# A fused attention and gated-GLU kernel on one core: the whole order of work is replaced by another, with four buffers of exponentials fewer and two down-weight tiles more

## The chip, the core and the metric

The kernel runs on one core of a Trainium2 chip. A core has five engines that run their own instruction queues side by side: TensorE (PE in the profile, its weight loads apart as PEld), VectorE (DVE), ScalarE (ACT), GpSimd (POOL) and SyncE (SP), which here issues the DMAs. The metric is the time of one execution on the device in microseconds, lower being better.

## The reference

For 2,048 tokens of width 512 the kernel computes two branches of the same input `x` and mixes them with a gate per token:

```python
g = sigmoid((x * gate_w).sum(-1, keepdims=True))
# branch a: 32 heads of 16, one shared key head and one shared value head
q = (x @ wq) as (32 heads, 2048, 16);  k = x @ wk;  v = x @ wv
p = softmax(q @ k.T * 16 ** -0.5)
a = (p @ v, heads side by side) @ wo
# branch b: width 1792 inside
b = (sigmoid(x @ w_gate) * (x @ w_up)) @ w_down
out = g * a + (1 - g) * b
```

## The kernel before, in words

**Tiling.** The tokens are cut into 4 blocks of 512 and the heads into 8 groups of 4, so there are 32 *units* of attention (a block of queries, four heads). A unit has 16 *chunks* of 128 keys. Operands of most products are split into a high and a low part (the tiles with two halves, `hl`, `w`, `wd`, `x`, `qs`), so that three products of parts make one product of full accuracy.

**Kinds of work on TensorE.** Three kinds use only 64 of the 128 rows of the array, and two of them run at once, one on the top rows and one on the bottom rows:

- *maxima* (letter m, line 1139): scores of a part of the queries against 512 keys into one of 8 PSUM banks, from which VectorE takes the maximum of each row (line 1141). 64 of them make a unit.
- *scores* (s, line 1148): the scores of 128 keys for 512 queries, with the maximum subtracted in the product; ACT makes the exponential of the bank into a tile `p` (line 1150). 64 make a unit.
- *feed-forward steps* (f, line 1113): products of the gate, the up, the down and the attention's output weights, summed in a bank over several steps. ACT takes a gate bank out (line 1122), VectorE an up bank (line 1128), and the parts of the output are gathered either by VectorE (line 1070) or by ACT into a tile of its own (line 1089), which POOL then adds (line 1092).

Three kinds use all rows of the array:

- *values* (V, line 1012): the four exponential tiles of one chunk times the values, summed in a bank over the chunks that follow one another. When a run of V ends, ACT copies the bank out (line 1019); if it is not the first run of the unit, POOL adds the copy to the unit's sum (line 1026).
- *projections and transposes at the start* (G, lines 870 and 943), and *turning the maxima* (T, line 998).

The maxima run some units ahead of the scores, and the feed-forward steps fill the rest.

**What sets the order.** The string `ORDER` lists all of TensorE's work by hand, one character a step. V, G and T are full-array steps. A hexadecimal digit is a pair of half-array steps: its upper two bits are what the top rows do, its lower two what the bottom rows do (0 nothing, 1 a maximum, 2 scores, 3 a feed-forward step). So `e` is a feed-forward step on top and scores below. A dot is a moment of waiting. `State.step` reads a character and emits the instructions:

```python
if code in "VGT":
    if not self.full:
        self.now += IN
    self.full = True
    ...
else:
    if self.full:
        if self.sum is not None:
            self.release()
        self.now += OUT
```

`release` is the end of a run of V: it emits the copy of the sum and, for a later run of the unit, POOL's addition. Which bank a step takes, when weights are loaded and split, and which engine gathers a part follow from clocks that `State` keeps for each engine, in units of which a pair takes 100. The constants are the paces of that model: `RED` is a maximum on VectorE, `EXP` an exponential on ACT, `COPY` and `SCALED` copies on ACT, `LATE` and `LATE_A` the time from a matmul to the start of VectorE or ACT on its bank. They do not reach the chip; they decide only what is emitted when. In the built program each engine carries its instructions out in the order in which they were emitted, and waits on semaphores for what it needs.

`PB` is the number of `p` tiles; `can_s` lets no score be issued while that many exponentials are held, and each V gives four back. `DB` is the number of `wd` tiles, which hold split down weights, attention-output weights and, at the start, parts of the third block of `x`.

Of the kernel before, what the change touches and what calls it, by code (L numbers as in the profile page):

```python
# [680 lines left out]


ORDER = (
    "GGGGGGG555G55G555.G55........5G55GG555GGG555G55G555GG55G557G777fddfffdffdfd7GT7dffff7ffd75Gdefffdfe7edef6f6f9fbf"
    "7b7b7bbdfedef97bf9fbffeeaaVV555VVV7b7b7bfbdedbdbf9fededededbf7bfb76fef67effd9VVVV5b7b7bfbfe7eeddbf6fedeedef7f6fe"
    "7bdbdbf6fbf5VTVV555VVVV7b7bb7fedbdbde7bfededeedef7e7fedb7bbd7bffd6V569VV97fbdbb7f9fe7ef6fbdededee7fb7f6f9fb7edef"
    "f75VVV59aVV97fbe7dbfbdbf6f9fbdededee7fe7f9f9fbdffd7775VVTVV655VVV76fef97efedee7f6f9fb7b7bbdfdbfb7edbdbfefed5VV56"
    "6VVV5bfbf97bf6fbf9f9fededeedef77e7bfb7be7ffddd5VVVV7b7bb7b7fededef9fe7edeede7ff6f9fe7e7bf9fbfaTV5a5VVVV5bbb77fef"
    "9fbdef6dbfedeede7f7efe7edb7eff7775VV599VV595VVV5eeedfbdf6fb7edbfbdb7bb7bdff97bfef9fe7edfd5VV566VVVdededefe7e7e7b"
    "dbfb7b7b7bbdfedf6feedf9ff7775VTVV596VV9dfbf6bdfb7bdbf9ef7ededee7ff6fed6febffb7bb9V555VVVVV5e9ffef6fbdef6e7bdfb7b"  # L690
    "7bbdfedfb79feed7bffd6V695VV569VV5a5VTVdedeedfe7e7e7bbdfb7b7b7bbfddbfbd6fede7efbfaV599VV5bb7fbb7fe7eedf9f6fededee"
    "f7b7fed6fe7dfd7777VVV599VV5ededefefb7e7e7bfbdb7b7bbdfedf9fbede7ff75f5VVVV966V5efeedbfb77b7bfedbddd7TVV999V9b77bf"
    "fededeedb7fefbb5VV566VV695VV5bfbf6f9f6fbde7b7efededee7fedbf76fbbdbfdbf5VV659TVV5eedfe7bfe7bf6dedbfb7b7bbfdf6f9f9"
    "fef6fedf75VVVVVVV7b7bbddef9fb7e7efbdeeeded7ffe7bf6fede7b7f5bV995VV5bbfbd7efb7bdef9fe7ededee7ff6fbdb7ebdf7ff56VVV"
    "TVVde5eefbdfb7afd7bfed7b7bbbfd7bedf6fedefb7fd6V595VVVVV7bdef9f6fb7ef97bfbdedeede7f7bf6f9fee7fbdbfaV5aaVV569VV959"
    "VV97bfb7f6f9feb7defe7edeede7ff6bfde7efb5bffa7TVV59aVVVVVV5efbf6defedb7b7edefb7bb7bfdf9fb7bdeedf6ff5dVVV5bb7bfb7f"
    "bd6fef9fededeeddfb7bbf76fef6fbfee6V9a9VV5a9VVVV5b7bbfefdb7af7defbdedeede7fb7f6fb7bf6fed9fdV555VVTVV97b7bff6f9fb7"
    "eedf6fedeede7ff67bfedefe7f7776VV999VVVV9dfeed7bfb7eededfb7b7b7bbdfedfb79fef6def7f5VVV555VVVdedeedfe7e7bf97efb7bb"
    "7b7bdf7bfb7b7eeeddfdddVTVVV5bbfdbf6f9fb7bf9efdeddeedbfb7b7fe7e7beffed5VVVV7b7b7bfededb7bf9fedededee7f7bf6fbb7f6d"
    "effd5VVV566VV5eefdef6fbdbf97ef9fb7b7bbfddbfe7b7bdefedbddTVV665VV569VV5b7bbff6fedef97bf6fdedeeef77efbde7bf9fe77d7"  # L700
    "VVVVVV5efededbfb7ef9f6fe7b7b7bbfddeedf9fef9fb7bfaV569VV699VVV5bb7fef6fede7ededbfb7bb7bfd7ebdf6fef9fbdfe5V566VV95"
    "6TVV595VVV79b7bfdef9fb7be7fededeedef77ee7f9fbbdf6fbfaV656VVV5efedbf9f9fbf6f6edfb7bb7bfdf9efde7bb7fdfdd5VV665VVVT"
    "V7b7bdbdef6fbf9edbf7ededee7ff67bfedefefb797bVVVdedefe7b7b7b7bfbdeefd5VV6ddefefb7b7b7bf9fefed9VVVVVV7b7edbdbfe7ed"
    "edef6fb7b7b7fedbfbd9fbf5ffddd5VVV677b7bfbfedef9dbfe7eeddedbfbf7b7b7bfedede7dTV665VV566VV9a6VV5eeddefefb76fbdbfe7"
    "b7b7bbfddef9fedbf6bf7fd9V56aVVVV5efe7edef6fbf97ef9fb7b7b7fededef6fdfbdb7bf5VVV595VVV59effbf6f6f9fef6defb7b7b7bfd"
    "bfed9fe7bffded6V569VTV659VVVVde7bf97ef9fb7e7bbfdededeef77bbdf6fbf6defbfaV5a9VVV97bfb7b7fed9fbf6fedededeef7e7f6f9"
    "fe7bfdf775VVTV5a5VV95aVVV59bffbe7f9fe7bbdfe7ededee7f7eefde7bf6fbfbb6VVVV5ededefbf9fef6f6fb7b77bbbdfdeedfbdee7fbf"
    "b76V9a6VV6aaVVV959VV9dfbf6def6f6fef9fe7b7b7b7efedfed9fbdfff7755VVVTVV5ededefbfed9fb7efb7b7b7bbdfedf9f9fe7bff57dd"
    "VV569VV67fedbbdfe7ede7efe7bb77bbfdf9f9fbbd7efedfd5VVVVVV5bbb77fef9f6fff9fededeed7efb7af7def9fff7755VVVV7b7bb7bdf"
    "bdee7dbfedededee7fb7fb7b7ef9fedfd5VVTVV7b7bb5fef9fbf6edef7ededee7f7efb7bde7bfedf79V5aaVV56aVVV566VV5ededefbf9fee"  # L710
    "7f9fb7b7b7bbfddeefedfb79fff575VVVV5efbdef6f9f6fedbf9fb7b7bbfdedfb76fedefdf779VTVVV5eededeffe7b7b7ef9fb7b7bbfdf9e"
    "f7bdbf6fdddf6VVV566VVV97bfbd7efbdbbd7eef7ededeef7f9fb7af7bd7effe5V96aTV569VV596VVV96aVV6eddeefdfb7bedf6fb7b7b7b7"
    "efededfedef9bf7bbbV966VVVV5eededfbfed6fbbdfb7b7bb7bdfdbf6fedbedfe7f75VVVV5b7bfedefedeed7be7fb7b7bbdfdbdbfafedf7d"
    "7f5dVVVV699V9b77bffededeed7bf6f77dTVV659VV977bfbfededede7bfefbb6V655VVVV7b7b5bfef9fbf9f9fedededeef77ee7fb7bdb7ef"
    "fd5VV5a5VV5efee77efbdbf9f6def7bbb7bfdb7fbde7eedfbfee5VTV566VVVV5ededefbf6fedbb7fe7b7b7bbdfdefededbf9fb7f76V959VV"
    "956VVV5bbfed7bf9fbe7dbf6fededeef77bfb7bdbdbfefed5VVVTV977bb7fef6fbbdbdfededeede7f7ef6fb7e7bfbdfd6V5a5VVVVV5b7bfe"
    "def9fe7bb7bdfededee7fe7efde7ef9bbf777VV596VVVV5edefef9f6f9fef6fb7b7bb7bdfedfed9fe7bbfd9f7V596VV59aVVVV7b7b7bf9f9"
    "fee7edf6fedeede7f7efedbdbb7fff575VTVV5efedb7bf9fafd7efedb7b7bbdfbdbf7e7ef9fefee6V9a9VV69aVV659VV97b7fbf9fe7be7ed"
    "e7fedeedef7e77bfb7b77fdddddVVV595TVVVV7b7bdeb7f9fef6dbf6fedeedef7f9bf7e7bedbfdf75VVV7b7bbdf9fedbf6f9ffedededb7bf"
    "b7b7be7fedefed5VVVVVV5bb7bf7bfed6fbf6fededeedef7b7fede7ebfd7f775VVTV995VVVde6fb7bdfbd6fef6defb7b7bbfdf9fe7edbedf"  # L720
    "efbb5VVV6dfb7bf9fb7bbd7edefedeedef7f6e7fe7bfddd777bVV959VVVV67bfeddef6febdf6fbdb7b7bbfdf6edfbf9fb6ffee9V596VTVVV"
    "VV5b7b7bfef9f9fbf6fedededee7fe77bf6fedefb75f7VVV6dedfeedfb7bdbe7fbdb7bb7bdfdbfedb7ef6fbdfd5VVVVVV5efef6f6fbdbf6f"
    "9efdb7b7bbfdb7dbfbdef6efdfd6V656VV956VVd9fbf6e7fedef6defb7b7bb7bdfbdfed6fbf9fe7efaTV595VVVVV5bfedb7efb7ede7efedb"
    "7bb77fbdef9f9fef9f6ff5eV665VVVV5ededefbfed6fb7bf9fb7b7bbdfbde7f9febd7efee7VTV99aVV5a9VVV5b7bfbfededede7efbfbabVV"
    "6a6VVVV7b7bbfdedededef6fbb7f5VV7b6fdbdefb7bbdf6fe7ededeef7e7edf6fbfbdb7bbeV9a9VVVV696VV5eedef7ef9fb7bf6edfb7bb7b"
    "fddbbfd6fbfbfeede6VaaaTVVVVVVfbbfeffbbfeeeeeeffffffbbffffbaffeabfeVVbbbbffffbfaaVVaaeeVVeeaaVVaaaVVaaaVVa.aaVVaa"
    "VaaVV...............Vcccccccccccc"
)


# [516 lines left out]
```

## Time and profile before

| | |
|---|---|
| median of 3 runs | 1588.57 us (1587.4 to 1588.57) |
| the profiled execution | 1589.17 us, of which the span from first to last instruction is 1587.0 us |
| granted TensorE clock | 0.999 |
| TensorE busy | 1578.4 us, 12,950 matmul records |
| VectorE busy | 1357.7 us, of which maxima 1256.0 |
| ACT busy | 1233.2 us, of which exponentials 1035.4 |
| POOL busy | 788.7 us |

The page of the profile gives each engine's busy time and the chain of work that ended last. The grouped lines name a line of the kernel, the engine and the operation, the tiles out and in with their shapes, the count, then the busy time, the mean length of one in ns, and the engine's idle time just before such instructions with what ended it. A row of the timeline gives the start, the length, the engine, the line and how many like instructions were merged. The matmuls of a pair overlap each other and the next pair, so lengths of matmuls do not add up; differences between starts do. In the program's records a V counts eight matmuls.

### The profile page before, as it was taken

Reading aid. Unit: us, or ns where it says so; the run is one execution under the profiler, and the core shown is the slowest. Engines: PE = TensorE matmul, PEld = TensorE weight load, DVE = VectorE, ACT = ScalarE, POOL = GpSimd, SP = SyncE. Lnnn points to the kernel's source line nnn. Section 1 sums busy time; section 2 is a strip of 40 time slices with the busy share of each in tenths; the row PEclk is TensorE's granted clock in tenths of the full one; section 3 lists DMA queues with packets and bytes.
Section 4 is the critical chain, followed back from the end, with each engine's and each line's share of the span. In section 5 each row is a group of like instructions: output and inputs, shape, how many; then the busy total and the mean of one; then the engine's idle time right before and its main releaser. Section 6 shows DMA issues by size and latency. Waiting matters only on the chain.

```text
span 1587.0 us, 33642 instructions
## 1 busy us (share of the span) xinstructions
PE 1578.4 (99%) x12950; PEld 1026.2 (65%) x12950; DVE 1357.7 (86%) x2320; ACT 1233.2 (78%) x2426; POOL 788.7 (50%) x662
## 2 busy tenths in 40 slices
PE   9999999999999999999999999999999999999998
PEld 7776666666666566666656666666666666676663
DVE  6989999999888889898998889888998988888751
ACT  4277787888778877887877978888887877787887
POOL 4253373657363455376463537274726346436432
PEclk9999999999999999999999999999999999999999
DMA  7422021122021221122121212022212122112011
GB/s 248 159 80 65 25 78 31 50 78 79 25 78 39 82 75 52 34 72 65 43 75 41 80 50 83 27 63 65 78 35 75 39 75 78 52 35 62 15 35 51
DMA packets 56000, 102.04 MB, mean 64 GB/s; under 512 B 16612, under 2 KB 18148, under 8 KB 55840
## 3 DMA queue, kind: packets, MB, share of 16 engines
q1 hardware_dynamic: 55840, 99.89, 20.3%
q8 instruction: 102, 1.67, 0.5%
q14 instruction: 58, 0.48, 0.1%
HBM read 78.11 MB, written 21.22 MB: 63 GB/s over the span
## 4 chain that ended last, share of the span: by engine, by line
PE 95%; ACT 3%; DVE 1%; SPq 0%; DMA 0%; issue 0%; POOL 0%; DVEq 0%; ACTq 0%
PE bank L1113 32%; PE bank L1012 29%; PE bank L1139 17%; PE bank L1148 14%; PE bank L870 3%; ACT p L1150 2%; SPq L986 0%; PE bank L998 0%; DVE mx L1141 0%; PE bank L1191 0%; DMA qs<-qd 0%; ACT x L796 0%; DVE x L802 0%; DMA wkv_raw<-wkv 0%; ACT q L965 0%
## 5 line engine op out<-in xcount | busy, mean ns | idle before, releaser
L1141 DVE TENSOR_REDUCE mx<-bank 128x1 f32<-128x512 f32 x2048 | 1256.0, 683 | 163.1 <-PE bank L1139 136.5
L1150 ACT ACTIVATE p<-bank 128x512 f32<-128x512 f32 x2048 | 1035.4, 665 | 4.9 <-PE bank L1148 1.0
L1148 PE MATMUL bank<-qs,ks 64*128 64x512 f32 x2048 | 725.8, 396 | 0.0
L1139 PE MATMUL bank<-ks,qs 62*128 62x512 f32 x2048 | 674.6, 409 | 0.2 <-DMA qs<-qd 0.2
L1012 PE MATMUL bank<-p,v_aug 128*32 128x512 f32 x4096 | 486.7, 597 | 0.3 <-ACT p L1150 0.3
L1139 PEld LDWEIGHTS bank<-ks,qs 62*128 62x128 f32 x2048 | 334.5, 184 | 152.7 <-issue 51.9
L1148 PEld LDWEIGHTS bank<-qs,ks 64*128 64x128 f32 x2048 | 361.9, 185 | 77.1 <-ACT p L1150 31.2
L1026 POOL TENSOR_TENSOR ou<-ou,ou 128x512 f32<-128x512 f32 x181 | 233.3, 1290 | 283.8 <-ACT ou L1019 277.2
L1019 ACT COPY ou<-bank 128x512 f32<-128x512 f32 x212 | 129.7, 612 | 279.4 <-PE bank L1012 136.5
L1113 PE MATMUL bank<-x,wu 64*128 64x512 f32 x1344 | 272.1, 391 | 0.3 <-SPq L1117 0.3
L1012 PEld LDWEIGHTS bank<-p,v_aug 128*32 128x32 f32 x4096 | 122.4, 109 | 230.1 <-issue 192.4
L1113 PE MATMUL bank<-wd,hl 64*128 64x512 f32 x1344 | 271.0, 391 | 0.0
L1113 PE MATMUL bank<-x,wg 64*128 64x512 f32 x1344 | 269.2, 391 | 0.0
L1113 PEld LDWEIGHTS bank<-x,wu 64*128 64x128 f32 x1344 | 201.5, 185 | 18.3 <-issue 1.7
L1113 PEld LDWEIGHTS bank<-wd,hl 64*128 64x128 f32 x1344 | 200.3, 185 | 17.0 <-issue 0.8
L1113 PEld LDWEIGHTS bank<-x,wg 64*128 64x128 f32 x1344 | 199.4, 185 | 16.8 <-issue 1.2
L845 POOL CAST wg<-rg 128x1024 fp32r<-128x1024 f32 x27 | 28.1, 1039 | 137.8 <-PE bank L1113 64.2
L1092 POOL TENSOR_TENSOR ba<-ba,pa_d 128x512 f32<-128x512 f32 x29 | 36.8, 1282 | 83.8 <-ACT pa_d L1089 83.8
L845 POOL CAST wu<-ru 128x1024 fp32r<-128x1024 f32 x27 | 28.1, 1041 | 97.8 <-PE bank L1113 58.1
L772 POOL TENSOR_TENSOR wd<-rd,wd 128x512 fp32r<-128x512 f32 x56 | 72.3, 1291 | 4.5
L772 POOL TENSOR_TENSOR hl<-h,hl 128x512 fp32r<-128x512 f32 x56 | 72.0, 1286 | 4.5
L1113 PE MATMUL bank<-wa,o 64*128 64x512 f32 x360 | 70.0, 392 | 0.0
(82 smaller groups left out, 758.4 us busy)
## 6 DMA issues: line engine op xcount, KB each, us to landing
rg<-wg SPq DMA_DIRECT2D x28, 512.0 KB
ru<-wu SPq DMA_DIRECT2D x28, 512.0 KB
rd<-wd SPq DMA_DIRECT2D x28, 512.0 KB
qs<-qd SPq DMA_DIRECT2D x192, 64.0 KB
qd<-q SPq DMA_DIRECT2D x32, 256.0 KB
od<-ou SPq DMA_DIRECT2D x31, 256.0 KB
xf<-x_in SPq DMA_DIRECT2D x16, 256.0 KB
ra<-wo SPq DMA_DIRECT2D x8, 512.0 KB
```

The source lines that it names most:

```text
L772: lo.tensor_tensor(hl[:, 1, :], raw, f32(hl[:, 0, :]), op=ALU.subtract)
L845: nc.gpsimd.tensor_copy(WS[item][:, 0, :], raw)
L870: nc.tensor.matmul(ps, w[:, p, part(kc)], X[b, kc][:, q, :], start=i == 0, stop=i == 3 * KC - 1)
L1012: nc.tensor.matmul(ps[32 * j:32 * j + 32, :], v_aug[:, c, :], PT.pop((u, c, j)), start=start, stop=stop)
L1019: nc.scalar.copy(to, ps)
L1026: nc.gpsimd.tensor_tensor(SUMS[u], SUMS[u], PARTS_OF[u].pop(0), op=ALU.add)
L1092: nc.gpsimd.tensor_tensor(BA[b, t], BA[b, t], PA[b, t].pop(0), op=ALU.add)
L1113: ins = nc.tensor.matmul(banks[i], l, r, start=start, stop=stop)
L1139: nc.tensor.matmul(banks[i], qs_t[u % 3][r, pr, part(qt)], ks[r, kb * 512:(kb + 1) * 512], start=True, stop=True)
L1141: nc.vector.tensor_reduce(MX[u][:, pr, h, qt, kb:kb + 1], banks[i], axis=AX.X, op=ALU.max)
L1148: nc.tensor.matmul(banks[i], ks[r, part(c)], qs_t[u % 3][r, pr, :], start=True, stop=True)
L1150: nc.scalar.activation(p, banks[i], AF.Exp, scale=0.25)
```

## The change

Three things differ; no function is touched.

1. `ORDER` is another string, and with it the order of nearly everything that follows from it: which step shares a pair with which, where the runs of V lie, which bank a step takes, and where loads, splits and additions stand in their queues. The planner's rules are the same.
2. The model's constants that are read while the string is carried out: `RED` 260 to 256, `EXP` 208 to 204, `COPY` 210 to 207, `SCALED` 247 to 244, `LATE` 190 to 186, `LATE_A` 200 to 192.
3. `DB` goes from 4 to 6 and `PB` from 29 to 25. A `wd` tile holds twice the bytes of a `p` tile, so the memory stays as it was.

```diff
-RAW, WB, DB, PB, HB, BA_BUFS = 2, 2, 4, 29, 6, 4
+RAW, WB, DB, PB, HB, BA_BUFS = 2, 2, 6, 25, 6, 4
...
-LATE, LATE_A, FREE, FREE_A = 190, 200, 65, 60
+LATE, LATE_A, FREE, FREE_A = 186, 192, 65, 60
...
-RED, GATED, SUM, ENDS, PARTS, INVERSE, LOWER = 260, 258, 285, 60, 225, 70, 285
-EXP, COPY, SCALED = 208, 210, 247
+RED, GATED, SUM, ENDS, PARTS, INVERSE, LOWER = 256, 258, 285, 60, 225, 70, 285
+EXP, COPY, SCALED = 204, 207, 244
...
 ORDER = (
-    "GGGGGGG555G55G555.G55........5G55GG555GGG555G55G555GG55G557G777fddfffdffdfd7GT7dffff7ffd75Gdefffdfe7edef6f6f9fbf"
+    "GGGGGGG555G.55G555G5.5..5....G55GG555GG555GGddd5G5dffffffff7737777fffffffffddd.55G555GGTG555G57bffbffbbff6defede"
...
```

Counted over the two strings:

| | before | after |
|---|---|---|
| V, G, T | 512, 24, 32 | 512, 24, 32 |
| runs of V, G and T between pairs | 210 | 180 |
| digits (pairs, some with one half empty) | 4,256 | 4,257 |
| copies of a sum by ACT (L1019) | 212 | 181 |
| additions of sums by POOL (L1026) | 181 | 150 |
| parts gathered by VectorE (L1070) | 32 | 24 |
| parts gathered by ACT and POOL | 36 | 44 |

What that looks like on TensorE in the nineteenth unit, at the chunk 13 (a name `p_13_0_0` is the exponential tile of chunk 13; the four matmuls of a chunk are one V). Before:

```order
L1012 MATMUL bank_73<-p_13_0_0_12534,v_aug 32x512
L1012 MATMUL bank_73<-p_13_0_1_12584,v_aug 32x512
L1012 MATMUL bank_73<-p_13_1_0_12470,v_aug 32x512
L1012 MATMUL bank_73<-p_13_1_1_12580,v_aug 32x512
L1139 MATMUL bank_74<-ks,qs_109 128x512
L1139 MATMUL bank_77<-ks,qs_109 128x512
L1139 MATMUL bank_75<-ks,qs_109 128x512
L1148 MATMUL bank_72<-qs_108,ks 128x512
L1148 MATMUL bank_76<-qs_108,ks 128x512
L1148 MATMUL bank_79<-qs_108,ks 128x512
L1012 MATMUL bank_78<-p_14_0_0_12545,v_aug 32x512
L1012 MATMUL bank_78<-p_14_0_1_12601,v_aug 32x512
```

After:

```order
L1012 MATMUL bank_73<-p_13_0_0_12542,v_aug 32x512
L1012 MATMUL bank_73<-p_13_0_1_12502,v_aug 32x512
L1012 MATMUL bank_73<-p_13_1_0_12535,v_aug 32x512
L1012 MATMUL bank_73<-p_13_1_1_12492,v_aug 32x512
L1012 MATMUL bank_73<-p_14_0_0_12563,v_aug 32x512
L1012 MATMUL bank_73<-p_14_0_1_12515,v_aug 32x512
L1012 MATMUL bank_73<-p_14_1_0_12556,v_aug 32x512
L1012 MATMUL bank_73<-p_14_1_1_12509,v_aug 32x512
```

Before, three pairs (of maxima and scores) part chunk 13 from chunk 14, and chunk 14 begins a new sum in another bank; after, the two follow each other in one bank, and the pairs stand elsewhere.

The end of the program on TensorE, before:

```order
L1148 MATMUL bank_79<-qs_108,ks 128x512
L1148 MATMUL bank_73<-qs_108,ks 128x512
L1148 MATMUL bank_74<-qs_108,ks 128x512
L1148 MATMUL bank_75<-qs_108,ks 128x512
L1012 MATMUL bank_72<-p_13_0_0_20153,v_aug 32x512
L1012 MATMUL bank_72<-p_13_0_1_20156,v_aug 32x512
L1012 MATMUL bank_72<-p_13_1_0_20147,v_aug 32x512
L1012 MATMUL bank_72<-p_13_1_1_20150,v_aug 32x512
```

And after:

```order
L1148 MATMUL bank_74<-qs_108,ks 128x512
L1148 MATMUL bank_79<-qs_108,ks 128x512
L1148 MATMUL bank_78<-qs_108,ks 128x512
L1148 MATMUL bank_72<-qs_108,ks 128x512
L1148 MATMUL bank_77<-qs_108,ks 128x512
L1012 MATMUL bank_76<-p_12_0_0_20076,v_aug 32x512
L1012 MATMUL bank_76<-p_12_0_1_20048,v_aug 32x512
L1012 MATMUL bank_76<-p_12_1_0_20070,v_aug 32x512
L1012 MATMUL bank_76<-p_12_1_1_20044,v_aug 32x512
```

Before, three V (chunks 13 to 15) are left when the last score has been issued; after, four (chunks 12 to 15). Of the last twelve feed-forward steps (those of `we`, line 1113) all followed the last V before; now six stand ahead of these four V.

More of the change, by code (lines that the diff above doesn't have):

```diff
@@ L683 @@
 ORDER = (
-    "GGGGGGG555G55G555.G55........5G55GG555GGG555G55G555GG55G557G777fddfffdffdfd7GT7dffff7ffd75Gdefffdfe7edef6f6f9fbf"
[L685 to L727, printed above, removed]
+    "GGGGGGG555G.55G555G5.5..5....G55GG555GG555GGddd5G5dffffffff7737777fffffffffddd.55G555GGTG555G57bffbffbbff6defede"
@@ new lines @@
+    "ede7ef7ede7ef9fbfbb7b9V555VVV6ddefe7efe7edbf6fb7b7b7bbdfbd9fb7bdbfedefdd6V555VVV656VV6dedef7ef9f6febd7bfb7b7b7ef"
+    "edededbfb7bdbf9TVGV57dVVV79bff6bdf9f6fe7bf9fededee7ef76febdf6fb7ff579VV555VVVdedededbf6fb7be7dbfb7b7bbddef6fef6f"
+    "9fbf7f5d5.VVV595VVV7b7b7bbfdbdeedf6fbdedeede7fe7af7ed7bf6fff795VTV955VVV97bfdee7fedb7be7dbfbde4edb7bf9fb7bdbf6fe"
+    "ddd7dVVVV767bb7fbfedbde7bdefedeeddeedf6fe7b7bfe7f7775VVVVTV5edeedeff9f6fbbdbf7b7b7bbdf9fbde7b7bfeddddf5VVVVV767b"
+    "b7fef9f6fbdefbdedeede7fe7e7b7bdbfedff755VVVV7b7ef9f9f6f9fbb7defedeede7ef7edeb7e7fbd5f777VVTVVVde9dfef6f9fb7edefb"
@@ new lines @@
+    "7b7b7bbdf9f9fb7edbf9fedf5dVVVVV7e7b7edbfb79fb7efedededee7f6fb7edb7efb7eff55VVV965VVV5bfef9dbfb79fb7ef6fededee7fb"
+    "de7bbdf6fb7ffd69VVV569VVV5bb7fbdbfed6fbbdf6fedeede77efe7bf9f9f6fbff69TVV655VVVVdede6ffbdb7bde7efbdb7bb7bdfb7ef9f"
+    "6efdbdef7d6VVVVVdadf7b7efb79fb7ef9fedededebf76fe7eb7f6fbf9bdVV65aVV996VTV699V6deedf7bfb76..bf9f9ff7dd6VVV5eedfe7"
+    "bfb79..b7efe7bdedbVV656VVdedeededf6fb7b7ebf7b7b7bbdf9fbdbf97efe7ddf5dVVVV7b7b79fef6fede7bfbdedeede7f6fef97bf9fbb"
+    "7df5dTVV656VVVV97b7fef9fbde7bf6bdfededee77ef6febdf6f9fb7f79V9a6VVVVV5edeeef7f6f9fbedb7fb7bb7bdfbd9feb7bdf6fdedf5"
@@ new lines @@
+    "VVV565VVV7b79fbf9fe79fedbe7fededee7fb7edbf6f9f6fff796TVVVVVd6dedefefb7bde7efb7b7b7bbdfedede7edbf9fbb7bdVV655VVVV"
+    "dededee7fb7e7e7efb7b7b7bbdf9f9fbde7bf9fefdd6V6a9VV5aaVTVVV7b7b7bb7fbdededbfededeede7fe7e7b7eedfbdb7f57VV959VVV7b"
+    "7bed7bfed9fbe7f9fedeede7fe7e7bed7bf9fff755VVVV7b7b7bb7fed9fbdeedfededee7fe7e7ef9dbfb7ff575VVTVVVVded6eedff6fbde7"
+    "bb7fb7b7bbdedfbdbdb7ef9fe7fd5VVVV7b7b7b9ffedb7edbfededeede7fe7b7bbdf6f9feff55VVVVVV7b7b7bbdf9fede7befdedeede7fb7"
+    "b7bf9f6fe7edfd6V569VVTVV5eeeeddffe76fbbdfb7b7b7bbdf9fedb7bf9f6fedfd5VVV656VVV6b7fdbdef9fb7bbd7efededee7fe79fb7eb"
@@ new lines @@
+    "df6fff579VV96aVVVVdedeb7b7fed6fee7dbfb7bb77bbfd9fef9defe7ffd55TVVVVV7b7bf9e7f9fedeb7f9fededee7fb7b7ef6dbf9fe7f5d"
+    "VVVVV7b7bbdfe7edbf6dbf9fededee7fe7b7e7efbdbdbff6aV565VVVVVdededee7fb76fef9bf7b7bb7bdfbd9fbf6defedff795VV6aaVTV59"
+    "6VV5a6V5eedef7ef9f6fedbfb7b7b7bbdfbdedef97bfb7efed9VV569VV569VVV7b7b7b7bbdfedef9fededeede7f6f6fedb7bf9fbf75eV565"
+    "VVVV5edeedfefe7bed7bfb7bb7b7bfdbdbf97efedbf6dd7dVTVVV56aV5eef7efe7b7b7bdbfefeeededffb7b7bb7f9ffddd5VVV565VVV9adf"
+    "f7f9f6fedbf6fedb7b7bbdfbdb7ef9b7fedefee6V565VVVVTVdede7b7bf9fbdb7bf6fededee7dbf6fef6f9fbdb7bebVVVVVVdedeeddefe7e"
@@ new lines @@
+    "7bb7fb7b7b7bbdfedb7bf97efbdedf5eVVVVV7b79bb7ffbde7ef9fedededee7f6f6fe7edefbfbb7b9V555VVVV7b977bfefbdbf9defe7eedd"
+    "ee7f6fe7bbdfe79fff755VVTV595VVV7b7b79fbf9fedbdefe7ededee7f6fb7bf9def6f6fbf9VV595VVV7b7bb5fbfbde7bdeedfededee7e7f"
+    "6fbf9f6f9fb7f9dV66aVV569VVTVV9b7ff6f9fb7edbdbf6fededee7e7fedb7bb7f9fffd55VVVVV7b7b7bbdfedb7eedf9fededee7f6fb7bf6"
+    "dbfedff755VVVV7b79fedbf9fb7bed7efedeede7fe7e7bf9f9fbd6ff57VVVVVV5edefb7ef6fedebd7bfb7bb7bdfbde7bbd7ef9fedfd6VV56"
+    "5VVTV7bdeed7bf6fedeb7edfb7bb7bdbdfbde7bf6fedfef9aVVVVVV7b7b7b7bbfdedeede7fededee7fb7edbed7bf9fff755VVTV659VV5b7e"
@@ new lines @@
+    "fbdefb79fbbdf6fedeede7ef7edbf6e7f9fbfb75VVVVV5ededefef6fb7bdbf6fb7b7bbddbf9fbede7f9fffd55VVVVV67bb7fdef9fef67bbf"
+    "dedededbfbde7bf67bfb7eefe5VVVTVVV5eedfe7bfed6fe7bdbfb7bb7bdfbd9fb7ef6fbdedd7dVVV6a5VV7b7bb77bfed9fbedfededeede7f"
+    "6f6fbbdf6f9ffbf55VVV656VVVdededee7fe7bdbb7e7fb7bb7bdf9fedbdef6f9fbdf76V5a6VTV559VVV7b7edef9f9fb7bf6f9fedeede7ef7"
+    "e7ef9f9fb7efb7aV5aaVV965VV595VVV7b7b97fbfbd9fe7eefdededeedf6f6fbb7f9faf7f75dVVVVV7b7bb5fefed6fedefedbb77bbfd9fbd"
+    "e7bfedbf6ed7dVVTVVV5b7bfbfedededef6ff777aV595VV7bb7f9fededeedfb7e7be7V95aVV9b77fbedfbdbdedbb7fededee7b7fb7e7b7ef"
@@ new lines @@
+    "ededbf5VVVVV5b7b7bfbf9f6fedefe7eededef7e7ededbfe7b7f77b5TVV959VV599VV97b7fef9f6fb7bedfe7edeede7f6fedbf97bf9fff7a"
+    "9VVVVVV5eedef7efe7e7ef9fb7b7bb7bdf9fbdbf9f6fedeff55VVVV7b7b7bbdf9fef97efededeedef7b7bf67bfed6fffd55VVTVVVV5eedfe"
+    "7efe7bdedbfb7b7b7bbdf9f6fbf9f6fbdeed7eVVVVV5edeef7efbd6fe7efb7b7b7bbdf9fbdedbdef6fe7bd7V695VV965VV959VTV6def7ede"
+    "f6fbf97bdefb7bb7bdf6fbde7edbf6fbdf5dVVVVV7b7bb7bdfbdedbf6fedededee7f6fe7ef6defb7b7f75VVVV9deededff6fb7bdefb7b7b7"
+    "bbdf9fbdee7bdf6fff5d5VVVVTV7b7bdbdbfede7bf6bdfededee7fe7e7bf9defb7bdf76VVVVVVded6deeff6fb7edbfb7b7b7bbdf9fbdbf97"
@@ new lines @@
+    "bfedefee9V555VVVV7b7bb97ffe7edbf9fedededee7fe7b7e7edbfb7ffd5aVVV566VV59aVTV6ddbfe7efbd9fee7f6fb7bb7bdbfde7ebdedf"
+    "e7fbf55VVV569VVVde6dfe7bf9f6fef6dbfb7b7b7edbf9febdf6fedff795VVVVV7b7bdbf9fe79fef97efedeededb7f6fbb7defe7bf7d5VTV"
+    "VVdedee77bfe7edb7edbfb7bb7bdbfd9fbf6e7fbdedf5dVV656VVVV5bfef6edfb7edebd7efb7bb7bdbdfbdb7be7fefedee9V565VVVVV5ede"
+    "fb7bfb79fbf9e7fededee7fe7ede7bfb7bfdf795VV659TVVVV7bdef9b7fe7bdeb7f9fedeede77efb7edbbdfb7eff69VVVVV97bbb7fdfedb7"
+    "ef6f9fedeede7f6fe7bdbdbfe7ff755VVVVVd6deefbdfb7bdef6f9fb7bb77bbfdbdee7b7fefeedaeVTV9a9VV669VVVV7b7bfbdedeededfb7"
@@ L728 @@
+    "e7be7V959VV7b7bbfdededeedfb7efb6bVVVdededeedfb76fbf6fb7b7.bb7bdfedbbdf67bf9fbedeeVV6aaVV669VVVVdedeedef7b7ef6b7f"
+    "9fb7b7bbdf9fedbf6ef79fbefeaVTVaaaVVVfefbaebffffabeVVVfefbeffefafbbaVVaaaVVaaaVVaaaV.Vbfbfbfbfeef.aeVVeeeefeffffb"
+    "ab.bVVbeeeccca888VVVVcccccc"
 )
```

## The prediction

> **What bounds the kernel now.** I read the page first, then the timeline of TensorE to price its work, then the grouped lines and the waits of the engines that empty its banks.
>
> ```profile
> PE 1578.4 (99%) x12950; PEld 1026.2 (65%) x12950; DVE 1357.7 (86%) x2320; ACT 1233.2 (78%) x2426; POOL 788.7 (50%) x662
> PE 95%; ACT 3%; DVE 1%; SPq 0%; DMA 0%; issue 0%; POOL 0%; DVEq 0%; ACTq 0%
> ```
>
> TensorE carries 95% of the chain that ended last, and the other engines are idle for 229 us (VectorE) and 354 us (ACT) of a span of 1587.0. A busy share of 99% says little by itself, because matmuls overlap; what a step of TensorE costs must be read from the spacing of its starts. These are starts of one stretch, in which the V steps (values, L1012, eight records each) and the paired half-array steps alternate, and behind them the count of matmuls in a stretch that holds pairs alone:
>
> ```profile
> 699.40 1.06 PE L1012 MATMUL bank<-p,v_aug 128*32 128x512 f32 x8
> 701.30 2.78 PE L1012 MATMUL bank<-p,v_aug 128*32 128x512 f32 x24
> 704.01 0.49 PE L1139 MATMUL bank<-ks,qs 62*128 62x512 f32 x2
> 704.35:711.57 7.22, 7.22 (x64) 1.00 0.13 34
> ```
>
> The stretch counts 64 matmuls, two of which began at 704.01; 62 are 31 pairs in 7.22 us, **0.233 us a pair**. Three V last 2.78, one lasts 1.06: **0.86 us a V**. From 699.40 to 701.30 lie one V and three pairs (the order has them so), 1.90 us, which leaves 1.90 - 0.86 - 3 x 0.233 = **0.34 us for one trip out of the pairs into the V and back**; 704.01 to 704.35 shows a part of it, 0.34 for the first pair where 0.233 is usual. The rest of the program by its own rows:
>
> ```profile
> 9.43 11.05 PE L870 MATMUL bank<-x,wq 128*128 128x512 f32 x48
> 20.32 0.60 PE L943 MATMUL bank<-consts,vt 128*128 128x128 f32 x4
> 20.67 3.02 PE L870 MATMUL bank<-x,wkv_s 128*128 128x512 f32 x12
> 77.50 0.41 PE L998 MATMUL bank<-consts,mm 128*32 128x128 f32 x2
> 77.84 0.73 PE L1113 MATMUL bank<-x,wg 64*128 64x512 f32 x2
> 1576.71 0.66 PE L1177 MATMUL bank<-consts,ou_last 128*128 128x128 f32 x4
> ```
>
> Sum for the kernel before: 9.4 us until the first projection is done; 19 more projections at 10.89 / 4 = 2.72 (9.43 to 20.32), 51.7; 4 turns at 0.35, 1.4; 32 maxima turned at some 0.22 (0.34 less the way back), 7.0; 512 V at 0.86, 440.3; 4,256 pairs at 0.233, 991.6; 210 trips at 0.34, 71.4; and 10.3 from 1576.71 to the end. Together 1583.1 of 1587.0. **Only 3.9 us are left for all waits of TensorE.** So nothing can be won by shorter waits; the time falls only if TensorE gets less to do, and rises if the new order makes it wait.
>
> **The change part by part.** *Fewer trips.* The letters of the table give 210 runs of V, G and T before and 180 after; V (512), G (24) and T (32) are as many as before. 30 trips at 0.34 are **-10.2 us**. All of it lies on TensorE, which has no spare time. Paired steps go from 4,256 to 4,257: **+0.2**.
>
> *What goes with the trips.* Each run of V that ends inside a unit costs a copy on ACT and an addition on POOL.
>
> ```profile
> L1150 ACT ACTIVATE p<-bank 128x512 f32<-128x512 f32 x2048 | 1035.4, 665 | 4.9 <-PE bank L1148 1.0 <-PE bank L1139 0.7 <-PE bank L1113 0.3
> L1019 ACT COPY ou<-bank 128x512 f32<-128x512 f32 x212 | 129.7, 612 | 279.4 <-PE bank L1012 136.5 <-issue 61.6 <-POOL hl L771 17.9
> L1026 POOL TENSOR_TENSOR ou<-ou,ou 128x512 f32<-128x512 f32 x181 | 233.3, 1290 | 283.8 <-ACT ou L1019 277.2 <-PE bank L1113 2.3 <-DMA qs<-mt 2.0
> L1070 DVE SCALAR_TENSOR_TENSOR ba<-bank,gom,ba 128x512 f32<-128x512 f32 x19 | 13.6, 745 | 0.1
> L1089 ACT ACTIVATE pa_d<-bank,gom 128x512 f32<-128x512 f32 x29 | 20.0, 749 | 0.2 <-PE bank L1113 0.2
> ```
>
> 31 copies and 31 additions go: 31 x 0.61 = 19 us of ACT and 31 x 1.29 = 40 us of POOL. Eight sums of parts move from VectorE (L1070, 0.745) to ACT (L1089, 0.749) and POOL (1.28): 6 us off VectorE, 6 on ACT, 10 on POOL. Net ACT -13, VectorE -6, POOL -30, all on engines that idle more than that: 0 us in the sum.
>
> *Buffers.* 25 tiles of exponentials instead of 29: the planner issues a score only while fewer than 25 are held, and V is issued earlier on the same TensorE queue, so in the program after the semaphore value that an exponential waits for on TensorE is that of its own score matmul, as before. Cost 0; if the cover went, ACT would wait for a V, 0.86 us each time. Six down-weight tiles instead of four let POOL split weights earlier; POOL is idle half of the span: 0.
>
> *The start.* By the projections and pairs that stand ahead of it, the first feed-forward pair comes some 14 us sooner than now. Its weights have to be there:
>
> ```profile
> 47.09 2.40 POOL L846 TENSOR_TENSOR wu<-ru,wu 128x1024 fp32r<-128x1024 f32 x1 [0.97 <-ACT wu L836]
> 67.22 0.39 PE L1113 MATMUL bank<-x,wg 64*128 64x512 f32 x1
> ```
>
> Split weights lie ready at 49.5, and loads and splits up to there stand in the same order on SP and POOL after; 67.2 - 14 is 53. Cost 0, with over 3 us of cover.
>
> *The end.* Before, the last V wait for exponentials:
>
> ```profile
> 1570.02 1.92 PE L1012 MATMUL bank<-p,v_aug 128*32 128x512 f32 x16
> 1572.27 1.55 PE L1012 MATMUL bank<-p,v_aug 128*32 128x512 f32 x8 [0.34 <-ACT p L1150]
> 1573.75 3.03 PE L1113 MATMUL bank<-we,o 64*128 64x512 f32 x12
> ```
>
> Two V take 2 x 0.86; the third should have begun at 1571.7 and ended 0.97 later, and both came some 0.5 us late: **1.0 us**. After, the last five scores stand ahead of four V (2.6 us before the last of them), so this goes: **-1.0**. The last feed-forward steps need the output of unit 30, which comes over six DMAs:
>
> ```profile
> 1550.94 0.54 SPq L1034 DMA_DIRECT2D sd<-ou  x1
> 1569.38 1.28 POOL L772 TENSOR_TENSOR we<-re,we 64x512 fp32r<-64x512 f32 x1
> ```
>
> From the store to the split weights 19.7 us pass; by the pairs and V between, the order after leaves about 21.8 (22.5 before). Cost 0, cover 2 us.
>
> *The tighter paces.* The table was searched with a paired step of 100 units, and that is 0.233 us here. A maximum was reckoned at 260 units (0.606 us) and now at 256 (0.596); an exponential at 208 (0.485) and now at 204 (0.475). The trace:
>
> ```profile
> 85.16 9.05 DVE L1141 TENSOR_REDUCE mx<-bank 128x1 f32<-128x512 f32 x15
> 224.99 14.57 DVE L1141 TENSOR_REDUCE mx<-bank 128x1 f32<-128x512 f32 x24 [1.90 <-PE bank L1139]
> 209.34 10.89 ACT L1150 ACTIVATE p<-bank 128x512 f32<-128x512 f32 x22
> ```
>
> Less the last one's length (0.683 and 0.665), these are 0.598 and 0.604 for a maximum, 0.487 for an exponential. So before the order was slightly generous to VectorE and about right for ACT; after, each maximum comes 0.002 to 0.008 late and each exponential 0.012. From below that costs 0 (late results find their bank not yet wanted). From above, if neither idled: ACT has some 2,300 such instructions, 28 us. A row near to the truth is the number of pauses:
>
> ```profile
> DVE mx L1141 <- PE bank L1139: 136.5, 121, 4.8
> ACT ou L1019 <- PE bank L1012: 136.5, 82, 4.6
> ```
>
> VectorE starts afresh 121 times and ACT 82 times in these rows alone, after 1.1 and 1.7 us on average, so lateness adds up over a run of some 20 only: 20 x 0.012 = 0.24 us at its end. How much room is there? Six pairs (1.40 us) is the shortest distance at which a bank of scores is written again; 732 of the 2,048 come back at it before, 942 after. A score of the trace needs 1.1 of them:
>
> ```profile
> 84.11 0.40 PE L1148 MATMUL bank<-qs,ks 64*128 64x512 f32 x1
> 84.63 0.60 ACT L1150 ACTIVATE p<-bank 128x512 f32<-128x512 f32 x1
> ```
>
> Start to the exponential's end is 84.11 to 85.23, 1.12 us, and 0.28 remain for the signal back. So most of the lateness fits, and the end of a long run just fails. I take **+4 us**, as much again as the 3.9 that is left for waits before; the ends 0 and 28 stay for the range.
>
> Sum: -10.2 + 0.2 - 1.0 + 4 = **-7.0 us**. The profiled execution took 1589.17 (2.2 around its span of 1587.0), so it would take 1582.2; the median of the runs shown is 0.6 lower, and I predict **1581.5 us**.
>
> **The rivals.** *The banks come back late (slower).* The place is the middle of a long stretch of pairs, 44 before and much the same after, in which maxima and exponentials share eight banks; the price is the 0.012 us by which each exponential is late. If half of the 28 us reaches TensorE, -11.0 + 14 = +3, and 1592 us. It decides from 11 / 28, four tenths, on. For it speaks that tight returns grow from 732 to 942; against it the pauses, and that TensorE waits for only 3.9 us though about a third of the returns are tight already.
>
> *VectorE is the real bound, and TensorE only waits for it (same).* Then trips saved on TensorE become waits for maxima, and the time stays at 1588.6 within 0.2%, about what a measurement of this kernel can tell. VectorE is busy for 86%, and in the second unit of the new order its work is as long as TensorE's (48.6 against 48.8 us by the prices above). Against it: in the units after that, up to the thirtieth, it has 76 to 95% of TensorE's time, and it waits for TensorE in the row above for 136.5 us. The Trainium skill, page "Perfetto Trace Analysis", section "Identifying the Most-Contended Engine", would have TensorE's room judged by its weight loads and the most contended engine by the highest share: 65% for weight loads, 86% for VectorE, which makes VectorE the engine to relieve, and the sum by that rule would be 0 instead of -7.0. The trace disagrees as far as the 31 pairs at 0.233 go: the next pair starts as soon as the one before is through, and VectorE's pauses end with TensorE.
>
> *The gain is whole.* The tighter paces cost nothing: -11.0, 1577.6 us. It is the lower part of my forecast and no case apart.
>
> **How the numbers follow.** My forecast (a gain from trips, less a few us of waits) gets 0.77: every term but one is a count times a price of the trace. Late banks get 0.12, VectorE as the bound 0.11. Faster by over 0.2% (below 1585.4) is 0.77, within 0.2% 0.11, slower 0.12. The forecast's own range is 1574 (-11.0 and all 3.9 us of old waits gone too) to 1585.4 (waits of 8 us, twice what I take). The range for eight in ten reaches into both rivals: **1574 to 1590**.
>
> **What would show it.** Right: ACT has 181 copies L1019 and POOL 150 additions L1026; pairs stay at 0.233 us, V at 0.86; the waits for bank and exponential at 1572 are gone. Wrong: pairs of 0.25 or more in long stretches, with weight loads waiting for exponentials (L1150) or maxima (L1141) many times more often than before; VectorE's pauses before L1141 shrinking well below 136 us without a shorter span; or a wait for DMA before the last steps L1113.

## The result, and the profile after

The changed kernel takes **1601.64 us** (median, 1600.67 to 1602.46) against 1587.99 us for the kernel before in the same series: a ratio of 1.0086, with a 95% interval of 1.0069 to 1.0104. It is slower by 13.7 us; 7 us faster was predicted. The profiled execution has a span of 1600.3 us, 13.3 above the span of before, at a granted clock of 0.998.

First the page of the changed kernel: busy time, and the chain that ended last.

```profile
PE 1589.8 (99%) x12950; PEld 1030.8 (64%) x12950; DVE 1348.9 (84%) x2312; ACT 1218.1 (76%) x2403; POOL 758.2 (47%) x639
PE 96%; DVE 1%; DMA 1%; POOL 1%; ACT 0%; SPq 0%; issue 0%; DVEq 0%; POOLq 0%; ACTq 0%
```

Every engine beside TensorE has less to do than before, as foreseen, and the chain still runs through TensorE. On this page nothing is wrong, apart from 11.4 us more of busy TensorE with the same 12,950 matmuls. The grouped lines of the changed kernel say the same:

```profile
L1141 DVE TENSOR_REDUCE mx<-bank 128x1 f32<-128x512 f32 x2048 | 1249.8, 680 | 178.8 <-PE bank L1139 136.4 <-PE bank L1113 30.6 <-PE bank L1148 9.6
L1150 ACT ACTIVATE p<-bank 128x512 f32<-128x512 f32 x2048 | 1032.7, 692 | 6.0 <-PE bank L1113 1.1 <-PE bank L1148 0.9 <-PE bank L1139 0.2
```

One number has moved: an exponential lasts 692 ns where it was 665, with the same total busy time. ACT's instructions overlap, so a longer mean for the same sum means that more of them follow each other without a pause. The clear sign is in the waits, those of weight loads for a bank that ACT has to give back. Before:

```profile
PEld bank L1148 <- ACT p L1150: 31.2, 76, 0.8
PEld bank L1139 <- ACT p L1150: 33.9, 57, 0.8
PEld bank L1139 <- DVE mx L1141: 18.5, 27, 0.8
```

After:

```profile
PEld bank L1148 <- ACT p L1150: 39.0, 167, 0.8
PEld bank L1139 <- ACT p L1150: 37.2, 98, 0.8
PEld bank L1139 <- DVE mx L1141: 7.0, 11, 0.8
```

Weight loads wait for an exponential 265 times instead of 133, and those of L1139 for a maximum 11 times instead of 27. The sums in this view say little (a load that stands ready early is counted too). The counts point to ACT; the experiments below have to decide, since the counts mislead in one of them.

**Where the 13 us are.** The time of TensorE was taken apart by the spacing of its starts. Both kernels have some 85 stretches of 25 and more pairs in a row, nearly all of 43 pairs before and of 44 after. The mean from pair to pair leaves out the first step of a stretch, which comes out of a run of V and takes 338 ns in both kernels.

| in the profiled execution | before | after |
|---|---|---|
| mean from pair to pair in the long stretches | 232.3 ns (3,524 steps) | 236.3 ns (3,635 steps) |
| from the last pair to the first V of a run | 349 ns x 184 = 64.2 us | 396 ns x 161 = 63.7 us |
| from V to V in a run | 873 ns | 869 ns |
| start of the last pair | 1576.4 us | 1588.7 us |
| from there to the end of the span | 10.6 us | 11.6 us |

4.0 ns on 3,635 pairs are 14.5 us; 47 ns on 161 ways into V are 7.5 us. These **22 us of lateness** stand against the 10 us that the trips gave. In their sum the ways into V hide their part completely: 23 fewer of them, each dearer, and the sum comes out the same within 0.5 us.

One stretch shows how it comes about. The windows view of the changed kernel (length, TensorE's busy time with its count, clock) for 42 pairs, 0.2395 us each, and the row of ACT's timeline inside it:

```profile
459.08:469.14 10.06, 10.06 (x86) 1.00 0.17 53
460.58 9.41 ACT L1150 ACTIVATE p<-bank 128x512 f32<-128x512 f32 x19
```

ACT does 19 exponentials without a pause, (9.41 - 0.69) / 18 = 0.484 us each. TensorE issues a score at every second pair, 2 x 0.231 = 0.462 us. Each exponential falls behind by some 0.02 us. The room is the time from the end of an exponential to the next matmul on the same bank. By the records it is 255 ns at 461.4 us, and gets smaller at the tightest places: 205, 145, 134, 87 and at last 53 ns. The shortest in the whole trace is 52. There TensorE stops, in the timeline of the changed kernel:

```profile
466.69 0.42 PE L1148 MATMUL bank<-qs,ks 64*128 64x512 f32 x1
466.78 0.39 PE L1113 MATMUL bank<-x,wu 64*128 64x512 f32 x1
466.95 0.39 PE L1139 MATMUL bank<-ks,qs 62*128 62x512 f32 x1
467.10 0.18 PEld L1148 LDWEIGHTS bank<-qs,ks 64*128 64x128 f32 x1 [0.20 <-ACT p L1150]
467.10 0.50 PE L1148 MATMUL bank<-qs,ks 64*128 64x512 f32 x1
467.44 0.18 PEld L1148 LDWEIGHTS bank<-qs,ks 64*128 64x128 f32 x1
467.67 0.39 PE L1148 MATMUL bank<-qs,ks 64*128 64x512 f32 x1
```

The pair after 466.78 starts 0.32 us later, at 467.10, and the next one, whose weights are loaded at 467.44, another 0.34 us later. Each loses some 0.1, and then the room has to be spent anew. Over the whole program the room was below 0.1 us for 27 exponentials before and for 189 after.

The two strings tell why ACT was not behind before. In the long stretches of the old one 1,053 scores follow the one before after two pairs, and 67 after a rest of four; in the new one it is 1,151 and 21. Most of the rests in which ACT could catch up are gone, and ACT's records agree: in these stretches its next instruction follows an exponential at ACT's own pace (within 6 ns of the median, 478 and 477 ns) after 82% of the exponentials before and after 92% now. No run puts the rests back into the new order, so that they are the reason is read from the strings and the records, not tested by itself.

### The profile page after: what moved, and what is told of

Its sections match the earlier page's. It is cut to its first block, busy times and chain, and to the rows that moved or that the text cites. A ratio compares the mean times of both kernels' runs of the same rounds, so it can differ in the third digit from the quotient of the medians.

```text
span 1600.3 us, 33656 instructions
## 1 busy us (share of the span) xinstructions
PE 1589.8 (99%) x12950; PEld 1030.8 (64%) x12950; DVE 1348.9 (84%) x2312; ACT 1218.1 (76%) x2403; POOL 758.2 (47%) x639
## 4 chain that ended last, share of the span: by engine, by line
PE 96%; DVE 1%; DMA 1%; POOL 1%; ACT 0%; SPq 0%; issue 0%; DVEq 0%; POOLq 0%; ACTq 0%
PE bank L1113 33%; PE bank L1012 29%; PE bank L1139 17%; PE bank L1148 15%; PE bank L870 2%; DVE mx L1141 1%; DMA rd<-wd 0%; PE bank L998 0%; SPq L986 0%; PE bank L1191 0%; POOL wd L772 0%; POOL wg L846 0%; DVE q L966 0%; DMA qs<-qd 0%; ACT x L796 0%
## 5 line engine op out<-in xcount | busy, mean ns | idle before, releaser
L1141 DVE TENSOR_REDUCE mx<-bank 128x1 f32<-128x512 f32 x2048 | 1249.8, 680 | 178.8 <-PE bank L1139 136.4
L1150 ACT ACTIVATE p<-bank 128x512 f32<-128x512 f32 x2048 | 1032.7, 692 | 6.0 <-PE bank L1113 1.1
L1148 PE MATMUL bank<-qs,ks 64*128 64x512 f32 x2048 | 749.6, 403 | 0.0
L1139 PE MATMUL bank<-ks,qs 62*128 62x512 f32 x2048 | 696.9, 411 | 0.5 <-DMA qs<-qd 0.5
L1012 PE MATMUL bank<-p,v_aug 128*32 128x512 f32 x4096 | 480.3, 597 | 0.0
L1139 PEld LDWEIGHTS bank<-ks,qs 62*128 62x128 f32 x2048 | 341.5, 184 | 144.6 <-issue 61.0
L1019 ACT COPY ou<-bank 128x512 f32<-128x512 f32 x181 | 109.9, 607 | 308.0 <-PE bank L1012 164.4
L1026 POOL TENSOR_TENSOR ou<-ou,ou 128x512 f32<-128x512 f32 x150 | 193.2, 1288 | 288.7 <-ACT ou L1019 274.3
L1113 PE MATMUL bank<-wd,hl 64*128 64x512 f32 x1344 | 285.2, 394 | 0.0
L1113 PE MATMUL bank<-x,wu 64*128 64x512 f32 x1344 | 281.5, 394 | 0.8 <-SPq L1117 0.8
L1113 PE MATMUL bank<-x,wg 64*128 64x512 f32 x1344 | 278.2, 394 | 0.0
```

The lines of the kernel that those rows point to most:

```text
L1012: nc.tensor.matmul(ps[32 * j:32 * j + 32, :], v_aug[:, c, :], PT.pop((u, c, j)), start=start, stop=stop)
L1019: nc.scalar.copy(to, ps)
L1026: nc.gpsimd.tensor_tensor(SUMS[u], SUMS[u], PARTS_OF[u].pop(0), op=ALU.add)
L1113: ins = nc.tensor.matmul(banks[i], l, r, start=start, stop=stop)
L1139: nc.tensor.matmul(banks[i], qs_t[u % 3][r, pr, part(qt)], ks[r, kb * 512:(kb + 1) * 512], start=True, stop=True)
L1141: nc.vector.tensor_reduce(MX[u][:, pr, h, qt, kb:kb + 1], banks[i], axis=AX.X, op=ALU.max)
```

## The experiments

All are timed against the kernel before in the same series (medians 1588.5 to 1588.8 us there, and 1588.0 in the series of the changed kernel, so differences between series are good to about 1 us). Theory A: ACT gives the score banks back late. Theory B: VectorE does so with the maxima, or is the bound. Theory C: the pairs of the new order are slower on TensorE itself, or wait for weights.

### Shorter exponentials, in both orders

```diff
-        nc.scalar.activation(p, banks[i], AF.Exp, scale=0.25)
+        nc.scalar.activation(p[:, :448], banks[i][:, :448], AF.Exp, scale=0.25)
...
-            nc.tensor.matmul(ps[...], v_aug[:, c, :], PT.pop((u, c, j)), start=start, stop=stop)
+            p = PT.pop((u, c, j))[:, :448]
+            p = bass.AP(tensor=p.tensor, offset=p.offset, ap=[p.ap[0], [192, 2], [1, 256]])
+            nc.tensor.matmul(ps[...], v_aug[:, c, :], p, start=start, stop=stop)
```

V still streams 512 columns, 64 of them twice, so TensorE has the same work. (Lines behind this place stand two further down in these kernels: L1152 is the exponential, L1150 the score, L1141 the maximum's matmul, L1143 the maximum.)

> The changed kernel, but ACT makes the exponentials of 448 of a bank's 512 columns, and V still streams 512 columns (the first and the last 256 of those 448), so that TensorE's work is the same and each exponential on ACT is about 0.05 us shorter (0.478 to some 0.42 from start to start). The exponentials of 64 queries of each 512 are left out. Theory A (ACT returns the banks of scores late): most of the 20 us of new waits goes, 1576 to 1585 us instead of 1601.6. Theory B (VectorE's maxima are late): 1597 to 1602. Theory C (the pairs of the new order are slower on TensorE itself, or wait for weights): 1597 to 1602.

Measured: 1579.31 us, ratio 0.9942 (0.9927 to 0.9956). 22.3 us less than the changed kernel. Theories B and C had 1597 to 1602 and fall as the cause of most of the loss. Pairs in the long stretches come down from 236.3 to 232.6 ns and the way into V from 396 to 341, and weight loads wait for an exponential 27 times instead of 265:

```profile
PEld bank L1141 <- ACT p L1152: 16.8, 20, 0.8
PEld bank L1150 <- ACT p L1152: 5.3, 7, 0.8
```

> The same edit on the kernel before, as a control: its waits for ACT are few, so 1584 to 1588 us by all theories. If it fell as much as the changed kernel does, the edit would say nothing on the change.

Measured: 1583.23 us, ratio 0.9966 (0.9955 to 0.9978), 5.5 us less than before. That is a little below the 1584 to 1588 that was expected. A cut of the same length on ACT is worth four times as much in the new order. Theory A holds. The rest was a surprise: the new order is then only 3.9 us ahead of the old, and ten had been expected.

### Shorter maxima, in both orders

```diff
-        nc.vector.tensor_reduce(MX[...], banks[i], axis=AX.X, op=ALU.max)
+        nc.vector.tensor_reduce(MX[...], banks[i][:, :448], axis=AX.X, op=ALU.max)
```

> The changed kernel, but VectorE takes the maxima over 448 of a bank's 512 keys (64 keys of each 512 are left out of the maximum), about 0.07 us less for each. Theory A: 1595 to 1601 us, since banks of maxima are not those that come late. Theory B: 1576 to 1585. Theory C: 1597 to 1602.

Measured: 1601.3 us, ratio 1.0081 (1.0066 to 1.0096): no change. It lies 0.3 above theory A's range, and far from theory B's.

> The shorter maxima on the kernel before, as a control: 1585 to 1588 us by all theories.

Measured: 1587.41 us, ratio 0.9991 (0.9982 to 1.0): no change either. In the changed order VectorE was idle for 258 us before its maxima instead of 179, and nothing was gained by it. Theory B falls, as long as the exponentials keep their length.

### Both shorter

> The changed kernel with both the exponentials and the maxima over 448 of the 512 columns (an eighth of the scores is left out of both). With the exponentials alone cut, the changed order took 1579.3 us and the old one 1583.2: 3.9 us of the about 10 us that thirty trips fewer are worth. Theory: the missing 6 us are waits for VectorE, which comes next as soon as the exponentials are quick; then cutting the maxima too gives 1572 to 1575 us here. Rival: they lie where neither engine is late (the end, the weight transfers, the start); then it stays at 1578 to 1580 us.

Measured: 1574.01 us, ratio 0.9905 (0.989 to 0.992).

> The kernel before with both exponentials and maxima over 448 of 512 columns, as the partner of the run above. Both theories expect little below the 1583.2 us that the short exponentials alone gave: 1581 to 1583 us. Less than that would mean that the old order, too, waited for VectorE once the exponentials were quick, and the difference between the two orders is what counts.

Measured: 1581.84 us, ratio 0.9957 (0.9942 to 0.9972).

With the exponentials quick, the maxima come next: another 5.3 us in the new order, 1.4 in the old. The pairs show where: in the new order they go from 232.6 to 231.3 ns, 4.7 us over the 3,635, in the old from 231.6 to 231.4. The way into V stays at 341 and 340 ns, so the gain is not there.

With both short, the orders are alike in these two prices, pairs of 231.3 and 231.4 ns and ways into V of 340 and 341 ns. What is left between them is what the strings differ in. The last pair starts at 1559.6 us in the new order and at 1569.6 in the old: **10.0 us for thirty trips**, the price that the prediction had taken from the trace. Both cuts together move the last pair by 29.1 us in the new order and by 6.8 in the old; the 22.3 between them are the lateness of the table once more, measured another way. At the end of the run 7.8 us of it are left; the rest is below, under the end and the hardware.

### The constants, or the order

The constants enter the kernel by two doors: the string was searched with them, and the planner picks banks and engines by them. Here the new string runs with the old constants (and the new buffer counts), and the planner's assertion that a bank is free by its own clock is taken out.

```diff
-LATE, LATE_A, FREE, FREE_A = 186, 192, 65, 60
+LATE, LATE_A, FREE, FREE_A = 190, 200, 65, 60
...
-RED, GATED, SUM, ENDS, PARTS, INVERSE, LOWER = 256, 258, 285, 60, 225, 70, 285
-EXP, COPY, SCALED = 204, 207, 244
+RED, GATED, SUM, ENDS, PARTS, INVERSE, LOWER = 260, 258, 285, 60, 225, 70, 285
+EXP, COPY, SCALED = 208, 210, 247
...
         i = self.free.index(min(self.free))
-        assert self.free[i] <= self.now
```

> The changed kernel's order string under the paces of the kernel before (LATE 190, LATE_A 200, RED 260, EXP 208, COPY 210, SCALED 247), with the planner's assertion that a bank is free by its own clock taken out; the result stays the reference's. The constants then act only where the planner picks a bank, an engine for a sum or the moment of a task. Theory (the order itself is too tight): 1599 to 1604 us, as the change. Rival (the picks made with the tighter paces are at fault): near the old time, 1585 to 1592 us.

Measured: 1601.01 us, ratio 1.0075 (1.0059 to 1.0092). It is the order, and not the picks. By the old paces the new string takes a bank too early 769 times, and the old string never.

### How late is late

The same cut as above at 496 and at 504 columns.

> The changed kernel with the exponentials over 496 of the 512 columns, 16 fewer (a thirty-second of the scores is left out); cut by 64 columns it gained 22.3 us. Theory: each exponential is late only by some 10 ns against the plan, and lateness adds up over a stretch, so that a cut of some 13 ns gives most of it back: 1582 to 1588 us. Rival: the time follows the exponentials' length in proportion, since ACT is simply too busy in these stretches: 1601.6 less 16/64 of 22.3, that is 1596 us.

Measured: 1582.45 us, ratio 0.9959 (0.9944 to 0.9974).

> The changed kernel with the exponentials over 504 of the 512 columns (a sixty-fourth of the scores is left out). 16 columns fewer gave 19.2 us of the 22.3 that 64 gave. One exponential then starts every 471 ns instead of every 477 by the length of a column in those runs (0.8 ns), which is the planned 204 units at 2.31 ns. Theory (late against the plan): the pace that was planned is met, more than half of the loss comes back, 1584 to 1591 us. Rival (any cut gains by its length, 16 columns 19.2 us, so 8 columns half of it): 1592 us.

Measured: 1590.38 us, ratio 1.0013 (1.0003 to 1.0022).

| columns | start to start of back-to-back exponentials, median | beyond two pairs (462 ns) | time | pair / way into V |
|---|---|---|---|---|
| 512 | 477 ns | 15 ns | 1601.6 us | 236.3 / 396 ns |
| 504 | 471 ns | 9 ns | 1590.4 us | 234.2 / 376 ns |
| 496 | 464 ns | 2 ns | 1582.5 us | 232.9 / 352 ns |
| 448 | 443 ns (a tenth of them 424 or less) | none | 1579.3 us | 232.6 / 341 ns |

The first 16 columns give 19.2 us, the next 48 only 3.1, so the time does not follow the exponentials' length in proportion. The bend lies where the exponential's pace meets two pairs. ACT's busy share over the span does not show it: it is 76% with 496 columns as with 512. The long stretches do: with 512 columns 92% of the exponentials there are followed at ACT's own pace, with 496 columns 82%, as in the kernel before. What counts is the pace against the distance at which scores are issued. The run with 504 columns lies in its theory's range, but only 1.6 us from the rival's value, and does not tell the two apart by itself. It does show that the plan is not the measure: at 504 columns the planned 471 ns are met, and 496 columns are still 7.9 us quicker.

The weight loads after the exponentials, with 496 columns:

```profile
PEld bank L1150 <- ACT p L1152: 10.7, 30, 0.8
PEld bank L1141 <- ACT p L1152: 22.8, 32, 0.8
```

62 waits instead of 265.

The Trainium skill, page "ScalarE: Activation LUTs", section "Step-by-step: what each stage is for", gives 0.833 ns for an element of each lane. The runs agree: 16 columns shorten the pace by 13 ns, 0.81 ns each.

### The other half of the pair first

In a pair, the top half's matmul is always issued first. If that is the one that waits for a bank, the other half might wait behind it. The edit puts every feed-forward step of a pair first, also the few that begin a new bank.

```diff
-            for h, what in enumerate(divmod(int(code, 16), 4)):
+            for h, what in sorted(enumerate(divmod(int(code, 16), 4)), key=lambda k: k[1] != 3):
```

> The changed kernel with the two matmuls of a pair issued in the other order wherever one of them belongs to the feed-forward network and needs no new bank: that one first, the score or maxima matmul, which needs a bank, second. Theory: TensorE takes its instructions in order, so a late bank holds up the other half too; with the other half ahead of it, part of the 21 us of waits falls away: 1590 to 1598 us. Rivals: the next pair pays what this one saved, 1600 to 1603 us; or two matmuls of the same half now follow each other where the order flips, and the pairs overlap worse: above 1605 us.

Measured: 1603.18 us, ratio 1.0091 (1.0076 to 1.0106).

> The kernel before with the same turn of the two matmuls within a pair. Theory: with its 16 us of waits in all, a third of which are late banks, there is little to gain: 1584 to 1588 us. Rivals: no difference, 1588 us; or worse overlap of the pairs where the order flips: above 1592 us. If it gains, it would be a version faster than both kernels.

Measured: 1590.11 us, ratio 1.0012 (1.0003 to 1.0022).

A miss, twice: nothing is gained in the new order, and the old one is even 1.6 us slower. In the new order pairs of 236.3 ns and ways into V of 399 are those of the changed kernel, which fits the rival that the next pair pays what this one saved. Yet the view of waits had improved, in the changed order with this edit:

```profile
PEld bank L1148 <- ACT p L1150: 8.7, 15, 0.8
PEld bank L1139 <- ACT p L1150: 24.9, 36, 0.8
```

51 waits instead of 265, and not a microsecond gained. Here the order of two instructions decided which of them is seen to wait; the time from pair to pair is what the stretch costs.

No version faster than both kernels came out of it. The trips' 10 us showed only where ACT and VectorE had less to do. That an order which leaves ACT its 477 ns a score would keep them is an inference; none of the complete kernels tried here does both.

## Why the prediction was wrong

**Fewer trips, -10.2 us: right.** Counts are 181 copies and 150 additions, as read from the strings, and 10.0 us show at the last pair where neither engine is late. The changed kernel:

```profile
L1019 ACT COPY ou<-bank 128x512 f32<-128x512 f32 x181 | 109.9, 607 | 308.0 <-PE bank L1012 164.4 <-issue 65.1 <-POOL hl L771 22.1
L1026 POOL TENSOR_TENSOR ou<-ou,ou 128x512 f32<-128x512 f32 x150 | 193.2, 1288 | 288.7 <-ACT ou L1019 274.3 <-PE bank L1148 13.1
```

**What goes with the trips, and the buffers, 0: right.** ACT has 15 us less to do and is later all the same. For the buffers the trace speaks: ACT was idle for 6.0 us in all before its exponentials, and what ended the waits in that row are score, maximum and feed-forward matmuls, never a V that gives a tile back. No run changes the buffers alone.

**The start, 0: right.** The first feed-forward pair starts at 55.1 us, 12.1 sooner (14 had been reckoned), and its weights were split by 49.8.

**The end, -1.0: given back.** The wait for exponentials at 1572 is gone; the last four V run through in 3.64 us. But the sum's copy by ACT now holds up TensorE behind them, by as much, 1.04 us:

```profile
1583.82 3.64 PE L1012 MATMUL bank<-p,v_aug 128*32 128x512 f32 x32
1587.39 1.65 PE L1113 MATMUL bank<-we,o 64*128 64x512 f32 x6
1590.08 0.60 PE L1177 MATMUL bank<-consts,ou_last 128*128 128x128 f32 x3 [1.04 <-ACT ou_last L1175]
```

The step did not ask what covers that copy. Before, twelve matmuls stood between the last V and L1177, 3.03 us by the prediction's row; now there are six, 1.65.

**The tighter paces, +4 us: the step that failed. It measured 22.** The mechanism was named, and the ends of its range, 0 and 28, hold the value. The rest of the sum held: 10.0 us off by the trips and 22.3 on by lateness put the last pair 12.3 us later, and the wait behind it adds the last 1.0 of the 13.3. The +4 was taken as much again as the 3.9 us that the prediction had left for old waits; the two cuts took 6.8 out of the old order, so that base was low too. The size was wrong for three reasons.

- The lateness was said to add up over some 20 exponentials to 0.24 us and then to be forgotten in a pause, and 0.28 us of room was set against it. Both numbers were fair: the stretch at 459 us starts with 0.2 to 0.5 of room and has spent it after some 15 scores. But that makes the two *equal*, and where room and need are equal a stretch can fail at its end, and most do: 64 of the 87 stretches have pairs of 235 ns or more, against one of 86 before. The step concluded "most of the lateness fits".
- The exponential's pace was held against the planned 204 units. What it has to be held against is the distance at which the string issues scores, two pairs, 0.462 us. That could be counted in the string: scores at two pairs up from 1,053 to 1,151, and rests of four down from 67 to 21.
- A wait was priced by its own length inside a stretch. The way into V grew as well, from 349 to 396 ns, and there the lateness took 7.5 us. With shorter exponentials that way is back at 341. That a run of V, which uses both halves of the array, has to wait for the later one would explain it, and is not tested.

In its place: ACT, 3% slower than the distance at which it is fed (477 against 462 ns), cost nothing in the stretch at 459 us until some 15 scores had spent the room, and then pairs came late, the first two by 0.1 us each.

**The rivals.** "The banks come back late" is what happened; it had 0.12 and 1592 us, with half of 28 us reaching TensorE, where 22 of 28 did. What spoke against it, the pauses of ACT and the small waits of before, came from an order that had the rests. "VectorE is the bound" is rejected: an eighth off its maxima changed nothing while the exponentials had their length. So the rule of the Trainium skill, page "Perfetto Trace Analysis", section "Identifying the Most-Contended Engine", to relieve the engine with the highest share, pointed to the wrong one: VectorE was at 86%, but the engine whose relief counts is ACT, at 76 to 78%. Busy shares over the span alone could not tell.

**What would show it.** Weight loads that wait for exponentials many times more often was listed as the sign of being wrong, and it came, twice as often. Pairs of 0.25 us were listed too; the stretches have 0.236, and over their 3,635 steps that is enough. VectorE's pauses before L1141 (136.4 us) did not shrink.

## What to carry to other kernels

When an order written for one pace is replaced by a tighter one, compare the consumer's start-to-start time in long unbroken rows with the distance at which the producer feeds it, and divide the room by the difference. The result is the number of instructions after which the room is gone; a stretch that is as long fails before its end. A busy share over the whole span that is far from full says nothing about that: here 15 ns in 462 decided 22 us at a share of 76%. Price a stretch by the time from start to start, not by the waits that a view assigns.
